# Attention ahead of two expert layers on one Trainium2 core: the first batch entry's values and the written order of its attention

## The chip, the cores and the metric

One core of one Trainium2 chip. The metric is the device time of one execution in microseconds (us). The kernel's engines: TensorE multiplies matrices (PE in the profile; its weight loads are PEld), VectorE (DVE) and ScalarE (ACT) work on tiles in SBUF and PSUM, GpSimd (POOL) on SBUF alone, and SyncE (SP) issues all the loads and stores of this kernel, in one queue.

## The reference

Three parts follow one another; the change touches the first alone.

```python
B, H, S, D = 2, 8, 576, 64            # q, k, v: (B, H, S, D); factor 4, Sd = 144
q_d, k_d, v_d = means over groups of 4 positions
out_d = softmax(scale * q_d @ k_d.T) @ v_d          # coarse, repeated 4 times
mask = abs(i - j) < 4                               # a band of 7
out_local = softmax(where(mask, scale * q @ k.T, -1e9)) @ v
x = out_up + out_local                              # as (1152, 512)
# then: 8 experts, relu(x @ w1[e]) @ w2[e], weighted by a gate that is normalised
# 8 times by rows and columns; then softplus(h @ w_in) @ w_out, h the experts' sum
```

## The kernel before

**Attention.** A `Unit` is two heads of one batch entry; there are eight, four for each entry (b = 0, then b = 1). Each has four blocks: "c", the coarse attention, and 0, 1, 2, the local attention of three tiles of 64 queries each, every tile against its window of 72 keys. `units` lists them, and the loop over n at line 746 runs through the 32 blocks. For block n it emits the scores of block n, the transposes of the weights of block n - 2 (`turn`), and the products with the values of block n - 3 (`values`). The next unit's `setup` stands in the third and fourth block of a unit, the `load` of the unit after it in the fourth.

`load` (line 291) issues on SyncE the queries and keys of two heads (`qk`, one place, four loads), the local values by windows (`vw`, two places, four loads) and the values for the coarse part (`vd`, one place, two loads). `setup(g)` transposes three tiles on TensorE into a PSUM bank, sums groups of four on VectorE (line 327), and copies queries and keys to `flat`, `kT` and `fine`. For g = 0 GpSimd also adds the values of each group of four (lines 345 and 346) into `vs`. `scores` runs the matmuls, then VectorE takes the row maximum (374) and scales it (375), ScalarE takes three exponentials with their sums (379), and VectorE adds, inverts and multiplies (384 to 388). `values` runs the matmuls with `vs` (419) or `vw` (429), and VectorE adds both parts (444). When a unit of the first entry has its last block, `operands` makes from `xf` the seven operands for a dense product, each split in two parts of lower precision (240 to 242).

**Dense work.** `fetch_first` and `fetch_second` load a piece of w1 or w2 into `raw` (two places), and ScalarE, VectorE and GpSimd split it in two parts, with sums for a scheme of seven products in place of eight (111, 132 to 139, 153, 154). `first` is that product (line 606), `second` the second layer's (665). `beside` is the dense work of the first four steps on the first entry's rows; it is emitted among the second entry's blocks, from n = 19 on, 3600 columns a block. `hh` and `hl` hold the hidden layer and are first used there, two places each. After the attention comes the rest of the dense work, in which TensorE's order is written out by hand.

**Order.** Outside blocks marked `tc.manual_schedule(engines=...)` a planner chooses each engine's order from costs of its own; each engine then works through its list in that order. Inside, the engines named keep the order in which the program emits their instructions. The three stretches in the loop that belong to the first entry's attention are all the planner's: SyncE's loads, TensorE's matmuls, and the other engines' work.

Of the kernel before, what the change touches and what calls it, by code (L numbers as in the profile page):

```python
# [9 lines left out]
F32 = mybir.dt.float32  # L10
# [3 lines left out]
AF = mybir.ActivationFunctionType  # L14
# [6 lines left out]
def attention_moe_mlp(ctx: ExitStack, tc: tile.TileContext, q, k, v, w_gate, w1, w2, w_in, w_out, out):  # L21
    nc = tc.nc
# [13 lines left out]
    KD = DM // P  # L36
    SCALE = 1.0 / float(D) ** 0.5
    EPS = 1e-9
    NEG = -1e9 / SCALE

# [235 lines left out]
    class Unit:  # L278
# [2 lines left out]
        pairs = {}  # L281

        def __init__(self, n, b, u):
            self.b, self.u = b, u
            self.flat = flat[n % 2]
            self.state = {}

# [3 lines left out]
        def load(self, first=False):  # L291
            b, h0 = self.b, 2 * self.u
            self.qk = qk = ap.tile([P, NQ, 2, D], F32, tag="qk", bufs=1, name="qk")
            cuts = [slice(NB * g, NB * g + NB) for g in range(NB)] if first else [slice(0, NQ)]
            for cut in cuts:
                for w, src in enumerate((q, k)):
                    for hh in range(2):
                        nc.sync.dma_start(
                            qk[w * QT : (w + 1) * QT, cut, hh],
                            src[b, h0 + hh].rearrange("(t p) d -> p t d", p=QT)[:, cut],  # L300
                        )
            self.vw = vw = ap.tile([KW, NQ, 2, D], F32, tag="vw", name="vw")
            for t, w0 in ((0, 0), (NQ - 1, S - KW)):
                nc.sync.dma_start(vw[:, t], v[b, h0 : h0 + 2, w0 : w0 + KW, :].rearrange("h p d -> p h d"))
            for hh in range(2):
                src = v[b, h0 + hh, QT - R :, :]
                windows = bass.AP(tensor=src.tensor, offset=src.offset, ap=[[D, KW], [QT * D, NQ - 2], [1, D]])
                nc.sync.dma_start(vw[:, 1 : NQ - 1, hh], windows)
            self.vd = vd = ap.tile([HC, 2, 2, R, D], F32, tag="vd", bufs=1, name="vd")
            for hh in range(2):  # L310
                nc.sync.dma_start(vd[:, :, hh], v[b, h0 + hh].rearrange("(c p r) d -> p c r d", c=2, r=R))

        def setup(self, g):

            if g == 0:
                self.kT = ap.tile([P, NQ, QT], F32, tag="kT", name="kT")
                self.qkd = ap.tile([P, NQ, 2, QT // R], F32, tag="qkd", name="qkd")
            qkd = self.qkd
            tb = self.bank("tb", 1)
            tiles = slice(NB * g, NB * g + NB)  # L320
            for j in range(NB):
                nc.tensor.transpose(
                    tb[:, j * P : (j + 1) * P], self.qk[:, NB * g + j].rearrange("p h d -> p (h d)"), ident
                )
            tb = tb[:, : NB * P]
            tbv = tb.rearrange("x (t w p) -> x t w p", t=NB, w=2)
            nc.vector.tensor_reduce(  # L327
                qkd[:, tiles].rearrange("x t w g -> x (t w) g"),
                tb.rearrange("x (t g r) -> x t g r", g=QT // R, r=R), axis=AX.X, op=ALU.add,
            )  # L330
            for hh in range(2):
                half = slice(hh * D, (hh + 1) * D)
                nc.vector.tensor_copy(
                    self.flat[half, g, hh].rearrange("x (j g) -> x j g", j=NB), qkd[half, tiles, 0]
                )
            nc.scalar.copy(self.kT[:, tiles], tbv[:, :, 1])
            nc.vector.tensor_copy(fine[g][:D, :, 0], tbv[:D, :, 0])
            nc.scalar.copy(fine[g][D:, :, 1], tbv[D:, :, 0])
            if g:
                return  # L340
            vd = self.vd

            self.vs = vs = ap.tile([HC, 2, 2, D], F32, tag="vs", name="vs")
            for c in range(2):
                nc.gpsimd.tensor_tensor(vd[:, c, :, 0:2, :], vd[:, c, :, 0:2, :], vd[:, c, :, 2:4, :], op=ALU.add)
                nc.gpsimd.tensor_tensor(vs[:, c], vd[:, c, :, 0, :], vd[:, c, :, 1, :], op=ALU.add)

        def scores(self, blk):

            sc = self.bank("sc", 0)  # L350
            if blk == "c":
                rows, w, scale = 2 * CT, SD, SCALE / (R * R)
                for i in range(NB):
                    nc.tensor.matmul(
                        sc[:rows, i * w : (i + 1) * w], self.flat[:, i].rearrange("x h q -> x (h q)"),
                        self.qkd[:, :, 1], start=True, stop=True,
                    )
            else:
                rows, w, scale = P, KW, SCALE
                tiles = range(NB * blk, NB * blk + NB)  # L360
                nc.tensor.matmul(
                    sc[:, : NB * w], identb, mask[:, blk : blk + NB].rearrange("p t w -> p (t w)"),
                    start=True, stop=False,
                )
                for i, t in enumerate(tiles):
                    w0 = min(max(t * QT - R, 0), S - KW)
                    nc.tensor.matmul(
                        sc[:, i * w : (i + 1) * w], fine[blk][:, i].rearrange("x h q -> x (h q)"),
                        self.kT.rearrange("x t q -> x (t q)")[:, w0 : w0 + KW], start=False, stop=(i == NB - 1),
                    )  # L370
            scv = sc[:rows, : NB * w].rearrange("p (i s) -> p i s", i=NB)
            small = ap.tile([P, 3, NB, 1], F32, tag="small", bufs=4, name="small")
            mx, off, rs = [small[:rows, i] for i in range(3)]
            nc.vector.tensor_reduce(mx, scv, axis=AX.X, op=ALU.max)
            nc.vector.tensor_scalar(off, mx, -scale, None, op0=ALU.mult)
            ex = ap.tile([P, NB * SD], F32, tag="ex", bufs=3, name="ex")[:rows, : NB * w]
            ex = ex.rearrange("p (i s) -> p i s", i=NB)
            for i in range(NB):
                nc.scalar.activation(
                    ex[:, i], scv[:, i], AF.Exp, scale=scale, bias=off[:, i], accum_out=rs[:, i]  # L380
                )
            if blk == "c":

                nc.vector.tensor_scalar(rs, rs, EPS, float(R), op0=ALU.add, op1=ALU.mult)
            else:
                nc.vector.tensor_scalar(rs, rs, EPS, None, op0=ALU.add)
            nc.vector.reciprocal(rs, rs)
            nc.vector.tensor_tensor(ex, ex, rs.to_broadcast([rows, NB, w]), op=ALU.mult)
            self.state[blk] = ex
# [22 lines left out]
        def values(self, blk):  # L412
# [2 lines left out]
            pv = self.bank("pv", 2)  # L415
            if blk == "c":
                for hh in range(2):
                    for c in range(2):
                        nc.tensor.matmul(
                            pv[hh * D : (hh + 1) * D, :SD], self.vs[:, c, hh],  # L420
                            et[:, c].rearrange("s (i h q) -> s i h q", i=NB, h=2)[:, :, hh],
                            start=(c == 0), stop=(c == 1),
                        )
                self.xc = ap.tile([P, SD], F32, tag="xc", name="xc")
                nc.scalar.copy(self.xc, pv[:, :SD])
                return
            for i in range(NB):
                for hh in range(2):
# [27 lines left out]

    units = [Unit(4 * b + i, b, u) for b in range(B) for i, u in enumerate((0, 2, 1, 3))]
    units[0].load(first=False)

    wg = const.tile([P, 3, 2, E], F32, name="wg")  # L460
    nc.sync.dma_start(
# [277 lines left out]
    for g in range(NB):  # L739
        units[0].setup(g)  # L740
    units[1].load()
    LAG = 2
    DENSE = 3600
    side, columns = beside(), 0
    begin = len(stream) // 2 + LAG
    for n in range(len(stream) + LAG + 1):
        if n < len(stream):
            x, blk = stream[n]
            i, j = divmod(n, len(blocks))
            x.scores(blk)  # L750
            if j == 1 and 1 <= i <= 6:
                (fetch_first if i % 2 else fetch_second)((i - 1) // 2, (i - 1) // 2)
            if j >= 2 and i + 1 < len(units):
                for g in ((0, 1), (2,))[j - 2]:
                    units[i + 1].setup(g)
                if j == 3 and i + 2 < len(units):
                    units[i + 2].load()
        for lag, what in ((LAG, "turn"), (LAG + 1, "values")):
            if 0 <= n - lag < len(stream):
                x, blk = stream[n - lag]  # L760
                getattr(x, what)(blk)
        while columns < (n - begin) * DENSE:
            columns += next(side, 1 << 30)
    for _ in side:
# [99 lines left out]
```

## Time and profile before

| | us |
|---|---|
| median of 3 runs | 1100.37 (1095.17 to 1103.46) |
| the profiled execution's own time | 1101.04 |
| its span, first to last instruction | 1099.3 |
| TensorE busy | 1059.5 |
| VectorE busy | 731.5 |
| ScalarE busy | 555.6 |
| GpSimd busy | 540.4 |

Busy time is summed from the records of instructions. Those of TensorE overlap, so two records of 0.28 us can start 0.12 us apart; start to start tells what one costs. The clock column (PEclk) is the clock granted to TensorE in parts of 2.4 GHz: 1.00, or 0.50 for 1.2 GHz, or a mean of both.

### The profile page before, as it was taken

Reading aid. Unit: us, or ns where it says so; the run is one execution under the profiler, and the core shown is the slowest. Engines: PE = TensorE matmul, PEld = TensorE weight load, DVE = VectorE, ACT = ScalarE, POOL = GpSimd, SP = SyncE. Lnnn points to the kernel's source line nnn. Section 1 sums busy time; section 2 is a strip of 40 time slices with the busy share of each in tenths; the row PEclk is TensorE's granted clock in tenths of the full one; section 3 lists DMA queues with packets and bytes.
Section 4 is the critical chain, followed back from the end, with each engine's and each line's share of the span. In section 5 each row is a group of like instructions: output and inputs, shape, how many; then the busy total and the mean of one; then the engine's idle time right before and its main releaser. Section 6 shows DMA issues by size and latency. Waiting matters only on the chain.

```text
span 1099.3 us, 17902 instructions
## 1 busy us (share of the span) xinstructions
PE 1059.5 (96%) x6385; PEld 936.9 (85%) x6385; DVE 731.5 (67%) x1564; ACT 555.6 (51%) x1443; POOL 540.4 (49%) x569
## 2 busy tenths in 40 slices
PE   6699999999999999999999999999999998999998
PEld 5588878898987889888888988888898897889987
DVE  6999666565666676667667565766663578766765
ACT  4677644443444344434444443444443567676763
POOL 6745244565467576757765455354664212322321
PEclk9779989999999999999999999999999999999999
DMA  7545111211234335333443333223333273244112
GB/s 174 119 110 119 38 32 39 77 58 40 65 118 142 113 101 154 116 120 115 122 133 105 117 113 98 97 96 108 103 116 115 106 278 140 110 173 182 68 39 86
DMA packets 133497, 119.70 MB, mean 109 GB/s; under 512 B 35744, under 2 KB 111776, under 8 KB 133408
## 3 DMA queue, kind: packets, MB, share of 16 engines
q1 hardware_dynamic: 133408, 118.56, 35.0%
q8 instruction: 50, 0.82, 0.3%
q14 instruction: 39, 0.32, 0.1%
HBM read 93.11 MB, written 25.43 MB: 108 GB/s over the span
## 4 chain that ended last, share of the span: by engine, by line
PE 39%; POOL 5%; DMA 5%; DVE 4%; issue 3%; ACT 2%; SPq 0%; POOLq 0%; DVEq 0%; ACTq 0%
PE yps L665 20%; PE m L606 18%; DMA raw<-in_moe_w_out 2%; POOL sums L111 2%; POOL w2l L154 1%; POOL cva L188 1%; DMA raw<-in_moe_w 1%; POOL cva L197 1%; DMA raw<-in_moe_w_in 1%; DVE cva L178 1%; POOL w1l L139 1%; DVE cva L189 0%; DVE cva L179 0%; DVE cva L182 0%; ACT raw L196 0%
## 5 line engine op out<-in xcount | busy, mean ns | idle before, releaser
L606 PE MATMUL m<-xh,w1h 128*128 128x320 f32 (+1 forms) x1120 | 336.7, 301 | 13.2 <-ACT t L615 7.3
L606 PE MATMUL m<-xl,w1h 128*128 128x320 f32 (+1 forms) x1120 | 332.6, 297 | 0.0
L606 PE MATMUL m<-xh,w1l 128*128 128x320 f32 (+1 forms) x1120 | 332.2, 297 | 0.0
L606 PEld LDWEIGHTS m<-xh,w1h 128*128 128x128 f32 x1120 | 212.1, 189 | 38.8 <-ACT t L615 11.6
L606 PEld LDWEIGHTS m<-xl,w1h 128*128 128x128 f32 x1120 | 212.3, 190 | 12.0 <-DVE qkd L327 0.2
L606 PEld LDWEIGHTS m<-xh,w1l 128*128 128x128 f32 x1120 | 212.2, 189 | 0.3 <-issue 0.2
L665 PE MATMUL yps<-w2h,hh 128*128 128x512 f32 x502 | 198.6, 396 | 1.2 <-ACT hh L563 1.2
L665 PE MATMUL yps<-w2l,hh 128*128 128x512 f32 x502 | 198.2, 395 | 0.0
L665 PE MATMUL yps<-w2h,hl 128*128 128x512 f32 x502 | 196.4, 391 | 0.0
L665 PE MATMUL yps<-w2h,h 128*128 128x512 f32 x436 | 152.8, 392 | 0.0
L620 DVE TENSOR_TENSOR c<-m,t 128x256 f32<-128x256 f32 (+1 forms) x160 | 72.2, 452 | 98.1 <-PE m L606 96.7
L139 POOL TENSOR_TENSOR w1l<-sums,w1h 128x512 fp32r<-128x512 f32 x72 | 95.5, 1340 | 78.6 <-ACT w1h L138 57.7
L154 POOL TENSOR_TENSOR w2l<-raw,w2h 128x512 fp32r<-128x512 f32 x72 | 95.5, 1348 | 74.8 <-ACT w2h L153 74.8
L576 POOL TENSOR_TENSOR ab<-ab,up 128x320 f32<-128x320 f32 (+1 forms) x64 | 53.9, 843 | 157.9 <-ACT ln L572 114.5
L563 ACT ACTIVATE hh<-c 128x256 fp32r<-128x256 f32 (+1 forms) x138 | 60.1, 443 | 126.1 <-DVE c L620 123.4
L564 DVE SCALAR_TENSOR_TENSOR hl<-c,hh 128x256 fp32r<-128x256 f32 (+1 forms) x138 | 91.8, 671 | 35.3 <-ACT hh L563 33.3
L665 PEld LDWEIGHTS yps<-w2h,hl 128*128 128x128 f32 x502 | 94.5, 188 | 22.0 <-DVE hl L564 0.4
L665 PEld LDWEIGHTS yps<-w2h,hh 128*128 128x128 f32 x502 | 94.9, 189 | 13.7 <-ACT hh L563 1.5
L682 DVE SCALAR_TENSOR_TENSOR acc<-yps,pr,acc 128x512 f32<-128x512 f32 x117 | 86.9, 743 | 29.3 <-PE yps L665 29.2
L665 PEld LDWEIGHTS yps<-w2l,hh 128*128 128x128 f32 x502 | 94.9, 189 | 10.7
L665 PEld LDWEIGHTS yps<-w2h,h 128*128 128x128 f32 x436 | 82.2, 189 | 14.7
L188 POOL TENSOR_TENSOR cva<-cva,raw 128x512 uint32<-128x512 uint32 x32 | 42.8, 1338 | 95.1 <-DVE raw L185 76.6
(136 smaller groups left out, 1708.6 us busy)
## 6 DMA issues: line engine op xcount, KB each, us to landing
raw<-in_moe_w SPq DMA_DIRECT2D x72, 256.0 KB
raw<-in_moe_w SPq DMA_DIRECT2D x36, 512.0 KB
w1h<-s_in SPq DMA_DIRECT2D x10, 896.0 KB
w1l<-s_in SPq DMA_DIRECT2D x10, 896.0 KB
raw<-in_moe_w_in SPq DMA_DIRECT2D x32, 256.0 KB
raw<-in_moe_w_out SPq DMA_DIRECT2D x16, 512.0 KB
w2l<-s_out SPq DMA_DIRECT2D x10, 512.0 KB
w2h<-s_out SPq DMA_DIRECT2D x10, 512.0 KB
```

The source lines that it names most:

```text
L111: nc.gpsimd.tensor_tensor(sums[i], a, b, op=op)
L139: nc.gpsimd.tensor_tensor(lo[:, part], sums, hi[:, part].bitcast(F32), op=ALU.subtract)
L154: nc.gpsimd.tensor_tensor(lo[:, i], raw[:, i], hi[:, i].bitcast(F32), op=ALU.subtract)
L178: nc.vector.tensor_scalar(a, high, 0x07FFFFFF, 3, op0=ALU.bitwise_and, op1=ALU.logical_shift_left)
L188: nc.gpsimd.tensor_tensor(a, a, low, op=ALU.add)
L563: nc.scalar.activation(hh, c, AF.Relu)
L564: nc.vector.scalar_tensor_tensor(out=hl, in0=c, scalar=0.0, in1=hh.bitcast(F32), op0=ALU.max, op1=ALU.subtract)
L576: nc.gpsimd.tensor_tensor(ab, ab, up, op=ALU.subtract)
L606: nc.tensor.matmul(b[:, :h], x[:, i, kk, :], y[s][:, i, kk, :], start=(not more and n == 0), stop=(n == 5), skip_group_check=more,)
L620: nc.vector.tensor_tensor(c, b[:, :h], t, op=ALU.add)
L665: nc.tensor.matmul(y, a[:, f, tok], b[:, f, :], start=(start and m == 0), stop=(stop and m == 5))
L682: nc.vector.scalar_tensor_tensor(out=acc[t], in0=y, scalar=pr[:, t, e : e + 1], in1=acc[t], op0=ALU.mult, op1=ALU.add,)
```

## The change

The diff, cut to what changes the work:

```diff
-    NEG = -1e9 / SCALE
+    NEG = -1e9
 ...
 class Unit: load()
+            if b:
+                self.vd = vd = ap.tile([HC, 2, 2, R, D], F32, tag="vd", bufs=1, name="vd")
+            else:
+                vd = hp.tile([P, 4 * HALF[1]], F32, tag=("hh", "hl")[self.n % 2], name="vd0")
+                self.vd = vd = vd[:HC, : 4 * R * D].rearrange("p (c h r d) -> p c h r d", c=2, h=2, r=R)
+            for hh in range(2):
+                nc.sync.dma_start(vd[:, :, hh], v[b, h0 + hh].rearrange("(c p r) d -> p c r d", c=2, r=R))
+
+        def load_windows(self):
+            b, h0 = self.b, 2 * self.u
             self.vw = vw = ap.tile([KW, NQ, 2, D], F32, tag="vw", name="vw")
 ...
-            self.vd = vd = ap.tile([HC, 2, 2, R, D], F32, tag="vd", bufs=1, name="vd")
-            for hh in range(2):
-                nc.sync.dma_start(vd[:, :, hh], v[b, h0 + hh].rearrange("(c p r) d -> p c r d", c=2, r=R))
 setup()
-                nc.vector.tensor_copy(
-                    self.flat[half, g, hh].rearrange("x (j g) -> x j g", j=NB), qkd[half, tiles, 0]
+                nc.vector.tensor_scalar(
+                    self.flat[half, g, hh].rearrange("x (j g) -> x j g", j=NB), qkd[half, tiles, 0],
+                    SCALE / (R * R), None, op0=ALU.mult,
                 )
-            nc.scalar.copy(self.kT[:, tiles], tbv[:, :, 1])
+            nc.scalar.mul(self.kT[:, tiles], tbv[:, :, 1], SCALE)
 ...
-            if g:
+            if g or not self.b:
                 return
 scores()
-            nc.vector.tensor_reduce(mx, scv, axis=AX.X, op=ALU.max)
-            nc.vector.tensor_scalar(off, mx, -scale, None, op0=ALU.mult)
+            nc.vector.tensor_reduce(off, scv, axis=AX.X, op=ALU.max, negate=True)
 ...
-                nc.scalar.activation(
-                    ex[:, i], scv[:, i], AF.Exp, scale=scale, bias=off[:, i], accum_out=rs[:, i]
-                )
-            if blk == "c":
-                nc.vector.tensor_scalar(rs, rs, EPS, float(R), op0=ALU.add, op1=ALU.mult)
-            else:
-                nc.vector.tensor_scalar(rs, rs, EPS, None, op0=ALU.add)
+                nc.scalar.activation(ex[:, i], scv[:, i], AF.Exp, bias=off[:, i], accum_out=rs[:, i])
+            nc.vector.tensor_scalar(rs, rs, EPS, None, op0=ALU.add)
 values(), coarse
-                    for c in range(2):
+                    terms = [
+                        (c, x) for c in range(2)
+                        for x in ([self.vs[:, c, hh]] if self.b else [self.vd[:, c, hh, r] for r in range(R)])
+                    ]
+                    for m, (c, x) in enumerate(terms):
 ...
-                nc.scalar.copy(self.xc, pv[:, :SD])
+                nc.scalar.mul(self.xc, pv[:, :SD], 1.0 / R)
 the loop
-    for n in range(len(stream) + LAG + 1):
+    def block(n):
+        i, j = divmod(n, len(blocks))
 ...
-            if j == 1 and 1 <= i <= 6:
-                (fetch_first if i % 2 else fetch_second)((i - 1) // 2, (i - 1) // 2)
+            for f, fetch in {
+                1: [(0, fetch_first)], 3: [(0, fetch_second)], 6: [(1, fetch_first)],
+                9: [(1, fetch_second)], 14: [(2, fetch_first)], 18: [(2, fetch_second)],
+            }.get(n, []):
+                fetch(f, f)
 ...
+        if j == 2 and 1 <= i < len(units) - 1:
+            units[i + 1].load_windows()
+
+    with tc.manual_schedule(engines={mybir.EngineType.PE, mybir.EngineType.SP}):
+        for n in range(begin):
+            block(n)
+    for n in range(begin, len(stream) + LAG + 1):
+        block(n)
         while columns < (n - begin) * DENSE:
```

For the first entry the values of the coarse part go to the places of `hh` and `hl`, one of four for each unit, and stay as loaded; the sum over a group of four happens in the PSUM accumulation, with four matmuls for each one of before, and the factor 1/4 in the copy behind. The second entry keeps one place and GpSimd's sums. The factor of the scores goes into the copies of the transposed queries' means and keys, and the maximum's sign into its reduction. Loads of windows are apart from `load` and stand in the third block of the unit before. The pieces of weights are fetched at blocks 1, 3, 6, 9, 14 and 18 instead of 5, 9, 13, 17, 21 and 25. TensorE and SyncE follow the written order in the first 18 blocks.

## Rows read from the trace of the kernel before

**Rows 1.** The page, part 1: busy time (share of the span) xinstructions.

```profile
PE 1059.5 (96%) x6385; PEld 936.9 (85%) x6385; DVE 731.5 (67%) x1564; ACT 555.6 (51%) x1443; POOL 540.4 (49%) x569
```

**Rows 2.** Windows of 20 us: length, each engine's busy time, granted clock, DMA.

```profile
0.00:20.00 20.00, 11.80 (x53) 10.38 (x54) 10.72 (x35) 8.55 (x32) 10.71 (x32) 1.00 0.81 175
20.00:40.00 20.00, 14.89 (x104) 11.97 (x104) 18.63 (x49) 14.66 (x55) 16.30 (x19) 0.88 0.55 136
40.00:60.00 20.00, 14.07 (x96) 11.71 (x95) 18.72 (x46) 10.44 (x42) 14.31 (x16) 0.59 0.57 109
60.00:80.00 20.00, 19.91 (x172) 17.07 (x171) 17.77 (x64) 14.48 (x63) 6.54 (x9) 0.77 0.61 133
80.00:100.00 20.00, 18.49 (x179) 16.17 (x178) 19.72 (x68) 16.58 (x65) 8.94 (x11) 1.00 0.40 89
...
140.00:160.00 20.00, 18.44 (x118) 13.47 (x117) 14.52 (x26) 9.51 (x30) 8.87 (x10) 0.83 0.04 13
```

**Rows 3.** Windows cut by unit (columns: PE, PEld, DVE, ACT, POOL, clock).

```profile
11.36:27.14 15.78, 13.42 (x61) 11.09 (x62) 13.82 (x36) 10.44 (x42) 9.78 (x13) 1.00 0.90 200
27.14:42.10 14.96, 11.51 (x92) 9.32 (x93) 13.59 (x41) 10.52 (x42) 11.47 (x13) 0.77 0.57 128
42.10:62.26 20.16, 14.23 (x98) 11.71 (x97) 18.92 (x43) 11.64 (x46) 14.52 (x18) 0.58 0.54 113
62.26:74.16 11.90, 11.81 (x96) 10.19 (x94) 10.99 (x42) 7.66 (x36) 3.65 (x6) 0.70 0.52 111
74.16:85.86 11.70, 10.78 (x116) 9.34 (x115) 10.32 (x41) 9.73 (x39) 2.63 (x5) 1.00 0.55 124
```

**Rows 4.** VectorE's groups by shape, 0 to 70.3 us.

```profile
L386 DVE TENSOR_SCALAR small<-small 128x3 f32<-128x3 f32 x9 | 6.5, 719 | 0.1
...
L375 DVE TENSOR_SCALAR small<-small 128x3 f32<-128x3 f32 x11 | 4.2, 390 | 0.0
...
L375 DVE TENSOR_SCALAR small<-small 96x3 f32<-96x3 f32 x4 | 3.8, 942 | 0.0
```

**Rows 5.** Lines 375 and 333, whole span: duration ns min/median/max.

```profile
L375 DVE TENSOR_SCALAR small<-small x32: 149/169/2455, 13.9 to 140.7; 128x3 f32<-128x3 f32 x24, 96x3 f32<-96x3 f32 x8
...
L333 DVE COPY flat<-qkd x48: 181/198/202, 8.3 to 122.9; 64x48 f32<-64x48 f32 x48
```

**Rows 6.** Timelines of DVE, POOL and PE, 47 to 52 us: start, length.

```profile
47.74 2.52 DVE L375 TENSOR_SCALAR small<-small 96x3 f32<-96x3 f32 x2
...
48.09 1.40 POOL L111 TENSOR_TENSOR sums<-raw 128x256 f32<-128x256 f32 x2
...
51.55 0.34 PE L361 MATMUL sc<-mask,identb 128*128 128x216 bf16 x1 [4.46 <-ACT ex L379]
```

**Rows 7.** GpSimd's groups by shape, 0 to 70.3 us: the value sums.

```profile
L345 POOL TENSOR_TENSOR vd<-vd 72x256 f32<-72x256 f32 x12 | 8.5, 726 | 12.7 <-DMA vd<-in_v 12.7
...
L346 POOL TENSOR_TENSOR vs<-vd 72x128 f32<-72x128 f32 x10 | 4.8, 488 | 0.2 <-PE pv L419 0.2
```

**Rows 8.** TensorE's timeline, 58 to 62 and 84 to 88.2 us.

```profile
60.26 1.24 PE L419 MATMUL pv<-etc,vs 72*64 72x144 f32 x8
61.43 0.86 PE L408 MATMUL tp<-ident,ex 128*72 128x128 f32 x3
...
84.86 0.72 PE L419 MATMUL pv<-etc,vs 72*64 72x144 f32 x8 [0.43 <-ACT fine L338]
85.51 0.39 PE L606 MATMUL m<-xl,w1h 128*128 128x256 f32 x1
```

**Rows 9.** Window of the first unit, line 419 alone: PE, PEld, clock, DMA.

```profile
11.36:27.14 15.78, 1.97 (x8) 1.05 (x8) 1.00 0.90 200
```

**Rows 10.** Waits in the first 150 us, GpSimd's and the SP queue's.

```profile
POOL vd L345 <- DMA vd<-in_v: 23.0, 7, 5.5
...
SPq L304 <- PE pv L429: 41.3, 6, 12.3
```

**Rows 11.** Window of line 606 alone: PE, PEld, clock, DMA.

```profile
70.30:82.00 11.70, 4.60 (x22) 3.15 (x22) 1.00 0.46 106
```

More of the change, by code (lines that the diff above doesn't have):

```diff
@@ L283, in __init__ @@
         def __init__(self, n, b, u):
-            self.b, self.u = b, u
+            self.n, self.b, self.u = n, b, u
             self.flat = flat[n % 2]
@@ L351, in scores @@
             if blk == "c":
-                rows, w, scale = 2 * CT, SD, SCALE / (R * R)
+                rows, w = 2 * CT, SD
                 for i in range(NB):
@@ L358, in scores @@
             else:
-                rows, w, scale = P, KW, SCALE
+                rows, w = P, KW
                 tiles = range(NB * blk, NB * blk + NB)
@@ L371, in scores @@
             scv = sc[:rows, : NB * w].rearrange("p (i s) -> p i s", i=NB)
-            small = ap.tile([P, 3, NB, 1], F32, tag="small", bufs=4, name="small")
-            mx, off, rs = [small[:rows, i] for i in range(3)]
-            nc.vector.tensor_reduce(mx, scv, axis=AX.X, op=ALU.max)
-            nc.vector.tensor_scalar(off, mx, -scale, None, op0=ALU.mult)
+            small = ap.tile([P, 2, NB, 1], F32, tag="small", bufs=4, name="small")
+            off, rs = [small[:rows, i] for i in range(2)]
+            nc.vector.tensor_reduce(off, scv, axis=AX.X, op=ALU.max, negate=True)
             ex = ap.tile([P, NB * SD], F32, tag="ex", bufs=3, name="ex")[:rows, : NB * w]
@@ L417, in values @@
                 for hh in range(2):
-                    for c in range(2):
+                    terms = [
[3 more added lines that the diff above has]
+                    for m, (c, x) in enumerate(terms):
                         nc.tensor.matmul(
-                            pv[hh * D : (hh + 1) * D, :SD], self.vs[:, c, hh],
+                            pv[hh * D : (hh + 1) * D, :SD], x,
                             et[:, c].rearrange("s (i h q) -> s i h q", i=NB, h=2)[:, :, hh],
-                            start=(c == 0), stop=(c == 1),
+                            start=(m == 0), stop=(m == len(terms) - 1),
                         )
                 self.xc = ap.tile([P, SD], F32, tag="xc", name="xc")
-                nc.scalar.copy(self.xc, pv[:, :SD])
+                nc.scalar.mul(self.xc, pv[:, :SD], 1.0 / R)
                 return
@@ L458, in attention_moe_mlp @@
     units[0].load(first=False)
+    units[0].load_windows()
     wg = const.tile([P, 3, 2, E], F32, name="wg")
@@ L741, in attention_moe_mlp @@
     units[1].load()
+    units[1].load_windows()
     LAG = 2
@@ L745, in attention_moe_mlp @@
     begin = len(stream) // 2 + LAG
-    for n in range(len(stream) + LAG + 1):
+    def block(n):
+        i, j = divmod(n, len(blocks))
         if n < len(stream):
             x, blk = stream[n]
-            i, j = divmod(n, len(blocks))
             x.scores(blk)
-            if j == 1 and 1 <= i <= 6:
-                (fetch_first if i % 2 else fetch_second)((i - 1) // 2, (i - 1) // 2)
+            for f, fetch in {
[3 more added lines that the diff above has]
+                fetch(f, f)
             if j >= 2 and i + 1 < len(units):
```

## The prediction

> **What bounds the kernel now.** I began with the busy shares. TensorE is busy 1059.5 of 1099.3 us [rows 1], so a change pays only where TensorE idles or runs at its lower clock. The table by 20 us says where: the idle time of the first five slices is 8.20, 5.11, 5.93, 0.09 and 1.51 us, 20.8 in all [rows 2], against 40 in the whole span. Apart from the wait for the first loads this is the first entry's attention, which the change rewrites.
>
> Then the same table cut by head pairs. I cut where the coarse scores (line 354) of each unit begin, so a row is the pace of one unit [rows 3]: 15.78, 14.96, 20.16 and 11.90 us for the first entry's four (62.8 in all), 11.70 for the next. In the first three VectorE is busy 13.82 of 15.78, 13.59 of 14.96 and 18.92 of 20.16 us: it sets the pace. GpSimd's busy time moves with the pace: 9.78, 11.47 and 14.52 us in the slow units, 3.65 and 2.63 in the two fast ones.
>
> Why GpSimd matters is seen in VectorE's groups by shape. The two tiny scalings of line 375 and the addition of line 386 write 3 columns and take 390, 942 and 719 ns on average [rows 4], while the median of line 375 is 169 ns and its longest 2455 [rows 5]. One of these waits can be read off: at 47.74 two of them take 2.52 us together, GpSimd runs sums from 48.09 to 49.49 with more behind, and TensorE sits idle for 4.46 us until the exponentials that want line 375's result are done [rows 6]. So a tiny VectorE instruction waits behind GpSimd, and TensorE behind it.
>
> The Trainium skill (SBUF — State Buffer, Who interferes with whom) names this: copies and tensor-scalar instructions that use two ports wait for GpSimd's whole instruction. The trace agrees (2455 ns against 169).
>
> **The change, part by part.** *Line 375 goes*, since the reduction of line 374 negates its maximum. In the first 70.3 us 15 of them take 4.2 + 3.8 = 8.0 us [rows 4]. Own cost is 15 x 0.169 = 2.5 us; 5.5 us is waiting. Part of the waiting will be met by the next instruction that GpSimd can block (lines 386, 388); I take half, 2.7 us, as met again. Gain on VectorE 8.0 - 2.7 = 5.3 us, bounds 2.5 and 8.0, over some 3.75 units: 1.4 us a unit.
>
> *GpSimd's value sums go* for four units: two of line 345 at 726 ns and two of line 346 at 488 [rows 7] are 2.4 us a unit, 9.7 in all (the other 4 and 2 in those rows are the second entry's, and stay). GpSimd's busy time in the four units is 39.4 us [rows 3]; 29.7 stay, weight splits above all, 7.4 us a unit. Pace against GpSimd's time: the mean of the fast two is 11.8 us at 3.1, of the slow three 17.0 at 11.9, a slope of 0.59 us per us. At 7.4 it gives 11.8 + 0.59 x 4.3 = 14.3 us. This slope holds part of the waiting that I counted with line 375, so I take 1.0 of the 1.4 us there: 13.3 us a unit, bounds 11.8 (the quiet units) and 15.0 (the fastest slow one).
>
> *TensorE takes the sums*: 16 matmuls for 4, so 24 records more a unit. Eight take 1.17 us from start to start at 60.26, at 1.2 GHz, and 0.65 at 84.86, at 2.4 [rows 8]: 0.146 or 0.081 each, 3.5 or 1.95 us a unit. While VectorE sets the pace this costs nothing; TensorE's idle time in the first 60 us covers it. Without cover it costs 7.8 to 14 us in four units. In the first unit there is no cover. The clock column reads 1.00 there, but eight such records took 1.97 us [rows 9], even more than at 60.26, so I read that stretch as 1.2 GHz. TensorE is busy 13.42 us in it; with 3.5 more, 16.9 us.
>
> *Four places for the values* end waits on GpSimd (23.0 us in the first 150 [rows 10]), which only fed the sums: nothing on the path. *The windows' loads* come three blocks later, in a written order. Now their issue waits 41.3 us for TensorE on the SP queue [rows 10]; behind it stand the next head pair's query and key, and the weights. In the written order the wait for the values matmul stands right behind that matmul; what is queued behind it is the next unit's load. I cost this at 0; if a load came late, the transposes would wait, for as long as the worst stall that the rows show, 4.46 us [rows 6].
>
> *The weight fetches* move to blocks 1, 3, 6, 9, 14 and 18. Their conversions cost ScalarE, VectorE and GpSimd what they did: 0. *The scale* goes into copies that are there already. The copy of line 333 becomes a tensor-scalar, six a unit. Line 333 took 181 to 202 ns in all 48 [rows 5], so GpSimd never blocked it, and I take the new form at the same time; at worst each waits as line 386 does, 719 - 169 = 550 ns [rows 4, 5], 3.3 us a unit.
>
> *The written order of TensorE*: its waits stand now where a planner put them. A block later or earlier is worth some us either way; the rows have no price for it but the stalls that it may add or end (idle 5.11 and 5.93 us per slice [rows 2]). I take 0, with 5 us to each side.
>
> *What is given back.* Before, 22 records of the dense first product ran between 70.30 and 82.00 in gaps of the attention [rows 11]: they are busy 4.60 us there, but overlap; 256 columns at 2.4 GHz are 0.107 us, 22 of them 2.3 us. I expect the written order not to take them in; they come later, at full price.
>
> **The sum**: 16.9 + 3 x 13.3 = 56.8 us against 62.8, 6.0 less; 2.3 given back; 3.7 us gained, since all behind is bound by TensorE and only shifts. The profiled execution took 1101.04 us, 1.7 of it outside the span; 1097.3 follows. It lies 0.67 above the median of the runs, so on their scale 1096.7. No change and 1% (11 us) can hardly be told apart here.
>
> **Rivals.** *TensorE takes VectorE's place at the lower clock.* The granted clock fell (0.77, 0.58) in the two units where TensorE was busy 11.51 of 14.96 and 14.23 of 20.16 us, and was 1.00 in the one where it was busy 10.78 of 11.70 [rows 3]; a unit of 13.3 us leaves it gaps again. At 1.2 GHz a unit needs 14.23 + 3.5 = 17.7 us, above 13.3. If half of the last three units runs so, they take 15.5 each: 16.9 + 46.5 = 63.4, 0.6 more and 2.3 given back, 1103 on the runs' scale. If all of it does: 16.9 + 3 x 17.7 = 70.0, 7.2 more and 2.3 given back, 1110. This is the case on the other side; it decides if the clock stays low past the second unit. For it: 24 more records a unit on an engine that is slow there. Against it: a TensorE that never idles was given 1.00 in the end (60 to 80 us: busy 19.91 of 20, clock 0.77, then 1.00) [rows 2].
>
> *The clock rises early and stays.* If the denser stream gets 2.4 GHz in the second unit and the long stalls as at 47 us are gone, the units run at the pace of the quiet two: 16.9 + 3 x 11.8 = 52.3, 10.5 less; if the dense records still find gaps, nothing is given back, and the hole at 140 to 160 us (1.56 us idle, clock 0.83 [rows 2]) closes: 12.1 us less, 1088.3. The Trainium skill (TensorE: Matmul & The Clock Gate, Part 1) speaks for this: "the default state is throttled, and activity releases the throttle." The trace agrees in the slices from 60 us on.
>
> *The change doesn't do what it says*: line 333 in its new form is blocked like line 386, 3.3 us a unit on VectorE. 13.3 + 3.3 = 16.6, sum 66.7, 6.2 more with what is given back: 1106.6. The Trainium skill (VectorE: DVE Perf Modes, Mode 2×_2P) puts copy and tensor-scalar under one condition, on where the operands lie and how they are cut; by it, the new form does as the copy did, and nothing is added.
>
> **How the numbers follow.** Forecast 0.40 (1096.7; own range 1091.7 to 1101.7, the 5 us of the written order to each side); TensorE the bound half of the time 0.20 (1103); low clock throughout 0.13 (1110); early clock 0.21 (1088.3); blocked line 333 0.06 (1106.6). With the same 5 us about the two far cases, the range leaves out their outer parts: 1085 to 1110. Faster by over 1% (under 1089.4): most of the early clock and a little of the forecast, 0.22. Slower by over 1% (over 1111.4): the outer part of the low clock and late loads, 0.10. Within: 0.68.
>
> **What will show it.** The distances of the coarse scores' starts: 17, then about 13 us. VectorE without line 375; line 374 as long as before; line 333 at 0.2 us; line 386 still long where GpSimd splits weights. GpSimd's busy time near 7.4 us a unit. The coarse values' matmuls at 32 records a unit, 2.6 us at 2.4 GHz or 4.7 at 1.2. The first dense records, now scattered from 70.30 on, begin near there again, in a closed stream. I am wrong if a unit takes over 15 us, if TensorE waits for a load, or if the stretch after 100 us changes by more than what I shift.

## The result, and the profile after

The changed kernel takes 1108.78 us (median of 20 runs, 1099.26 to 1116.04) against 1100.80 us for the kernel before on the same chip (20 runs, 1095.17 to 1104.64): a ratio of 1.0059, 95% interval 1.0041 to 1.0077. It is slower, by 8.0 us between the medians; I had predicted 4 us less. Ten of its runs lie between 1099 and 1107 us and ten between 1111 and 1116. The profiled execution is one of the lower ten: 1102.99 us, with a span of 1101.2 against 1099.3.

The page, parts 1 and 3, shows more on TensorE and less on the two engines that were relieved [rows 1]: 96 records of matmuls (two for each of 48) and 96 of weight loads more, VectorE 10 us and GpSimd 13 us less. The queue marked q8 instruction has 51 packets in place of 50; it matters below.

```profile
PE 1064.5 (97%) x6481; PEld 944.2 (86%) x6481; DVE 721.5 (66%) x1532; ACT 555.1 (50%) x1443; POOL 527.3 (48%) x553
...
q8 instruction: 51, 0.84, 0.3%
```

Windows by unit, cut at the starts of the coarse scores (now line 363), answer to [rows 3]:

```profile
10.49:27.58 17.09, 16.93 (x78) 15.16 (x78) 10.62 (x37) 11.05 (x42) 8.35 (x8) 1.00 0.93 193
27.58:44.52 16.94, 16.14 (x121) 14.01 (x120) 11.95 (x37) 10.65 (x42) 5.91 (x7) 1.00 0.29 61
44.52:56.86 12.34, 11.38 (x120) 9.91 (x119) 10.75 (x38) 10.21 (x43) 2.64 (x2) 1.00 0.61 140
56.86:70.21 13.35, 12.97 (x132) 11.48 (x132) 12.70 (x40) 11.60 (x46) 8.94 (x11) 1.00 0.79 177
70.21:83.41 13.20, 11.20 (x113) 9.23 (x111) 12.56 (x36) 8.95 (x39) 7.72 (x10) 0.98 0.65 153
```

The first four units take 59.7 us in place of 62.8. In the first two VectorE is busy 10.62 and 11.95 us and TensorE 16.93 of 17.09 and 16.14 of 16.94: TensorE is the bound now. Where that time goes is one row a unit in TensorE's timeline (start, length, with the row that follows):

```profile
20.60 7.04 PE L426 MATMUL pv<-etc,vd 72*64 72x144 f32 x32
27.58 0.80 PE L363 MATMUL sc<-qkd,flat 128*96 128x144 f32 x2
...
40.88 3.70 PE L426 MATMUL pv<-etc,vd 72*64 72x144 f32 x32
44.52 0.98 PE L363 MATMUL sc<-qkd,flat 128*96 128x144 f32 x6
```

The 32 records of the coarse values take 6.98 us from their start to the next row's in the first unit, and 3.64 us in the second: 0.218 and 0.114 us a record, where I had taken 0.146 and 0.081 from eight of them [rows 8].

A landmark splits the rest. The first matmul of the gates (tile lt), which weight the experts, stands where the attention is over. Tile lt, before (line 480) and after (line 489), with the third execution of the changed kernel, e6, below them in a fence of its own (duration ns, first and last start):

```profile
L480 PE MATMUL lt<-xh,wgs x16: 308/354/415, 147.4 to 157.7; 128*16 128x256 f32 x8, 128*16 128x320 f32 x8
```

```profile
L489 PE MATMUL lt<-xh,wgs x16: 276/300/313, 144.5 to 154.4; 128*16 128x256 f32 x8, 128*16 128x320 f32 x8
```

```profile
L489 PE MATMUL lt<-xh,wgs x16: 276/300/313, 155.9 to 165.7; 128*16 128x256 f32 x8, 128*16 128x320 f32 x8
```

The profiled execution reaches the gates 2.9 us ahead of the kernel before, close to the 3.7 us of the forecast. From there to the end of the span it needs 1101.2 - 144.5 = 956.7 us, and the kernel before 951.9. So two things have to be explained: why other executions reach the gates late, and why all three profiled ones lose some 5 us behind the gates, where the program has hardly changed.

### The profile page after: what moved, and what is told of

The parts are those of the page before. It is cut to its first block, busy times and chain, and to the rows that moved or that the text cites. A ratio compares the mean times of both kernels' runs of the same rounds, so it can differ in the third digit from the quotient of the medians.

```text
span 1101.2 us, 18049 instructions
## 1 busy us (share of the span) xinstructions
PE 1064.5 (97%) x6481; PEld 944.2 (86%) x6481; DVE 721.5 (66%) x1532; ACT 555.1 (50%) x1443; POOL 527.3 (48%) x553
## 4 chain that ended last, share of the span: by engine, by line
PE 38%; POOL 5%; DMA 5%; DVE 5%; issue 3%; ACT 2%; SPq 0%; POOLq 0%; ACTq 0%; DVEq 0%
PE yps L674 20%; PE m L615 18%; DMA raw<-in_moe_w_out 2%; POOL sums L111 1%; DMA raw<-in_moe_w 1%; POOL cva L188 1%; POOL w2l L154 1%; POOL cva L197 1%; DVE cva L178 1%; DVE cva L179 1%; POOL w1l L139 1%; DVE cva L189 0%; DMA s_out<-cva 0%; DVE cva L182 0%; DMA s_in<-cva 0%
```

## The experiments

Ratios are to the kernel before, run on the same chip. "Gates" is the first matmul of tile lt in the run's profile, "behind" the span less that.

### The order of the two heads, and the written order

**e1, the two heads in turn.** The change runs eight matmuls (sixteen records) for one head, then eight for the other; here they alternate. The sums are the same.

```diff
-                for hh in range(2):
-                    for m, (c, x) in enumerate(terms):
+                terms = [(c, r) for c in range(2) for r in range(1 if self.b else R)]
+                for m, (c, r) in enumerate(terms):
+                    for hh in range(2):
+                        x = self.vs[:, c, hh] if self.b else self.vd[:, c, hh, r]
```

> The changed kernel, with the coarse values' matmuls of the two heads in turn instead of one head's sixteen records after the other's. Theory A (the added matmuls cost more than priced, because one head's matmuls stand in a row and those of the other head, which write the other half of the output's partitions, can't run beside them): 32 records take about 2.0 us at 2.4 GHz and 3.9 at 1.2 instead of 3.7 and 7.0; the dense stream starts 6 to 9 us earlier than in the changed kernel; the median falls from 1108.8 to 1100 to 1103. Rival B (what is gained ahead of 160 us is lost again in the later stages, where the order of instructions is the same): the dense stream starts earlier, the median stays at 1106 to 1110.

Measured: 1098.11 us, ratio 0.9976 (0.9949 to 1.0002), some 9 us faster than the change by the ratios, and not to be told from the kernel before. TensorE's timeline of e1, the same 32 records at the lower clock and at the higher:

```profile
36.01 4.11 PE L423 MATMUL pv<-etc,vd 72*64 72x144 f32 x32
40.05 0.56 PE L363 MATMUL sc<-qkd,flat 128*96 128x144 f32 x1
...
49.57 2.18 PE L423 MATMUL pv<-etc,vd 72*64 72x144 f32 x32
51.68 0.36 PE L363 MATMUL sc<-qkd,flat 128*96 128x144 f32 x1
```

They take 4.04 and 2.11 us: 0.126 and 0.066 us a record, little over half of what they cost in a row. The heads write PSUM partitions 0 to 63 and 64 to 127; in turn, records of the two start in pairs (at 49.742 and 49.747, 49.864 and 49.870 in e1), while those of one head start one by one, 0.12 us apart (at 41.059, 41.181, 41.304 in the change; only where the two rows meet do they overlap, at 42.406 and 42.412). The Trainium skill (TensorE: Matmul & The Clock Gate, Why this matters for your kernels) says that small matmuls run concurrently when their outputs lie in distinct column groups (of 32 PSUM partitions there). The runs agree with halves of 64, and add that the order in the queue decides.

**e2, the planner's order in the changed kernel, and e8, the same with the heads in turn.** The written order is taken away; in e8 on top of e1's edit.

```diff
-    with tc.manual_schedule(engines={mybir.EngineType.PE, mybir.EngineType.SP}):
-        for n in range(begin):
-            block(n)
+    for n in range(begin):
+        block(n)
```

> The changed kernel without the written order of TensorE and SyncE in the first 18 blocks. If the written order costs the time: 1098 to 1102, units closer than 12 to 17 us. If it's the added matmuls (theory A): 1105 to 1112, the units no closer than in the changed kernel, since 32 records still take 3.7 us or more.

> The changed kernel with the two heads' matmuls in turn, and with TensorE's and SyncE's order left to the planner. Against the written order (1098.1 with the same matmuls): if the written order helps, 1100 to 1105; if it is neutral, 1097 to 1099; if it hurts, 1091 to 1095.

Measured: e2 1108.60 us, 1.0061 (1.0038 to 1.0084), as the change; e8 1106.24, 1.0037 (1.0024 to 1.0051). The written order is worth nothing with the heads in a row and some 7 us with the heads in turn (0.9976 against 1.0037; the two ran on different chips). The 5 us to either side that I allowed it did not hold for both.

### Parts alone

**e3, the small operations only**: the kernel before with the factor of the scores in the copies, the maximum negated in its reduction (line 375 gone) and the 1/4 in the copy behind. GpSimd sums the values and the planner orders.

```diff
-            nc.vector.tensor_reduce(mx, scv, axis=AX.X, op=ALU.max)
-            nc.vector.tensor_scalar(off, mx, -scale, None, op0=ALU.mult)
+            nc.vector.tensor_reduce(off, scv, axis=AX.X, op=ALU.max, negate=True)
```

> The kernel before, with only the scale and the negated maximum moved (line 375 goes, GpSimd's value sums, places, loads and order as before). If the waits of tiny VectorE instructions behind GpSimd set the pace of the first entry: units 1.0 to 1.4 us closer, the dense stream 3 to 5 us earlier, 1096 to 1098. If the gain is taken up later (rival B): dense stream earlier, time 1099 to 1102. If the waits only pass to the next instruction: no unit closer, 1100 to 1102.

**e4, TensorE's sums only**: the kernel before with the four places and the change's loop for the coarse values, heads in a row.

```diff
-            if g:
+            if g or not self.b:
                 return
...
+                    for m, (c, x) in enumerate(terms):
```

> The kernel before, with only the value sums of the first entry by TensorE and the four places for them. Theory A: GpSimd loses 2.4 us a unit, TensorE takes on 3.0 us a unit at 2.4 GHz and 5.8 at 1.2: 1104 to 1110. If GpSimd's relief outweighs it: 1094 to 1099.

**e7, all but TensorE's sums**: the changed kernel, with GpSimd adding the first entry's values again.

```diff
-            if g or not self.b:
+            if g:
                 return
...
-                        for x in ([self.vs[:, c, hh]] if self.b else [self.vd[:, c, hh, r] for r in range(R)])
+                        for x in [self.vs[:, c, hh]]
```

> The changed kernel, but the first entry's value sums are GpSimd's again (its four places, later windows, written order, moved scale stay). Theory A (TensorE's sums in a row are what costs): 1092 to 1097, as the small operations alone (1094.6) or better. If the written order or the later windows cost the time: 1099 to 1106.

Measured: e3 1094.63 us, 0.9953 (0.9930 to 0.9976), the fastest of all; e4 1109.89, 1.0085 (1.0055 to 1.0115); e7 1096.81, 0.9960 (0.9943 to 0.9976). So the small operations gain, more than any case that I had written down for them, and the sums on TensorE, heads in a row, cost more than that, as theory A says of e4 and e7. e4's windows by unit show TensorE as the bound of the first two:

```profile
11.35:28.43 17.08, 16.25 (x74) 13.88 (x73) 10.67 (x36) 9.84 (x41) 6.39 (x8) 1.00 1.07 205
28.43:45.05 16.62, 16.62 (x119) 14.55 (x119) 12.71 (x34) 11.02 (x42) 9.95 (x12) 1.00 0.52 101
```

In e3 the addition behind the exponentials, line 386 before [rows 4], takes 442 ns on average where it had 719, but the product behind it, line 388 before, takes 835 where it had 589. VectorE's groups by shape, 0 to 70 us, line 388 before and then e3:

```profile
L388 DVE TENSOR_TENSOR ex<-ex,small 128x216 f32<-128x216 f32 x9 | 5.3, 589 | 0.1
```

```profile
L382 DVE TENSOR_TENSOR ex<-ex,small 128x216 f32<-128x216 f32 x10 | 8.3, 835 | 0.1
...
L380 DVE TENSOR_SCALAR small<-small 128x3 f32<-128x3 f32 x11 | 4.9, 442 | 0.1
```

### The changed kernel's two levels

**e5 and e6, the changed kernel again**, one execution each.

> The changed kernel once more, for its profile: its executions fall into two groups, ten from 1099 to 1107 us and ten from 1111 to 1116. If this one is of the upper group: theory C (the lower clock lasts longer in the first entry's attention) has the gates' matmuls begin 8 to 11 us after the 144.5 us of the profile of the lower group, with more at 0.50 ahead of them; rival D (the later stages lose it) has them begin at 143 to 146 and the loss after 300 us.

> The same again, a third profile, to see an execution of either group: expectations as in the run before it.

Measured: 1107.56 us (e5) and 1114.74 us (e6). e5 lies between the two groups (gates at 147.3, 958.4 us behind). e6 is one of the upper ten's kind; its windows by unit:

```profile
10.12:23.82 13.70, 13.09 (x78) 11.97 (x78) 10.78 (x37) 10.34 (x41) 4.54 (x5) 1.00 0.98 186
23.82:42.29 18.47, 15.23 (x121) 12.93 (x120) 13.07 (x38) 11.00 (x44) 9.80 (x10) 0.76 0.65 147
42.29:62.81 20.52, 20.52 (x121) 17.94 (x120) 11.79 (x38) 10.59 (x42) 2.61 (x3) 0.50 0.40 79
62.81:80.55 17.74, 17.74 (x133) 15.84 (x133) 13.70 (x40) 12.63 (x48) 10.83 (x12) 0.68 0.37 89
```

Its units take 70.4 us. In the third TensorE is busy 20.52 of 20.52 us at a granted clock of 0.50, while VectorE needs 11.79. In the first profile that unit ran at 1.00 and took 12.34. The same program thus reaches the gates at 144.5 or at 155.9, and what differs is in which units TensorE's clock is up, much as theory C has it; why it differs from one execution to the next stays open. In the kernel before VectorE hid the lower clock in three units of four [rows 3]; its 20 runs lie within 10 us, the change's within 17.

### The loss behind the gates

The seven profiles so far with TensorE's sums need 955.5 to 958.4 us behind the gates; the kernel before needs 951.9, e3 950.2 and e7 954.4. In the changed kernel the loss is idle time of TensorE. Windows from the gates to the end, the kernel before and then the changed one, have it busy equally long (934.48 and 934.28 us):

```profile
147.40:1099.30 951.90, 934.48 (x5399) 831.46 (x5397) 611.24 (x1209) 461.83 (x1079) 464.26 (x466) 1.00 0.33 109
```

```profile
144.50:1101.20 956.70, 934.28 (x5404) 830.99 (x5400) 614.07 (x1211) 461.31 (x1080) 463.09 (x466) 1.00 0.33 108
```

It idles 17.4 and 22.4 us. Part of it can be read at 296 us. SyncE's queue (start, length of each issue), the kernel before and then the changed one:

```profile
299.70 0.34 SPq L216 DMA_DIRECT2D s_in<-cva  x1
300.09 0.45 SPq L217 DMA_DIRECT2D s_in<-cva  x1
301.20 0.36 SPq L215 DMA_DIRECT2D s_in<-sums  x1
```

```profile
296.29 0.34 SPq L216 DMA_DIRECT2D s_in<-cva  x1
296.68 1.70 SPq L217 DMA_DIRECT2D s_in<-cva  x1
298.43 0.46 SPq L215 DMA_DIRECT2D s_in<-sums  x1
...
q8 instruction: 1, 0.02, 3.6%
```

One issue takes 1.70 us in place of 0.45. The last line is from the table of DMA queues between 296.2 and 298.4 us: a packet of the queue marked instruction, 16 KB, which started at 296.71. In the kernel before that packet came at 295.64, ahead of the issues. What the late transfer holds up, in the changed kernel's timelines of GpSimd and of TensorE:

```profile
300.23 0.74 POOL L111 TENSOR_TENSOR sums<-raw 128x256 f32<-128x256 f32 x1 [2.47 <-DMA s_in<-cva]
...
306.89 0.39 PE L674 MATMUL yps<-w2h,hl 128*128 128x512 f32 x1
308.35 0.39 PE L615 MATMUL m<-xh,w1h 128*128 128x256 f32 x1 [1.07 <-DVE c L629]
```

GpSimd waits 2.47 us for the transfer, the weights' conversion is late, VectorE with it, and TensorE stands 1.07 us. The packets go with TensorE's records: 50 for 12770 before, one for each 255, so I take them for its program. The Trainium skill (Runtime: NRT & Kernel Launch, Instruction fetch mechanics) says that engines stream their instructions in blocks of 256, each crossing "mostly hidden". Here TensorE shows no idle time over 0.3 us in the 1 us behind any packet past the gates, but the transfer that starts with one is late. Behind the gates all six issues of the changed kernel that took over 0.3 us more than their kind (6.0 us in all), and both of the kernel before (1.6 us), have such a packet within 2 us; the packets come some 22 us apart.

The change adds 192 records ahead of all this, so all later packets fall elsewhere. e9 to e15 move them with matmuls that nobody reads.

**e9 to e11: padding in the first entry's units**, 8 a unit in e1's kernel (e9) and in the changed one (e11), 24 in e3's (e10).

```diff
+                if not self.b:
+                    for k in range(8):
+                        nc.tensor.matmul(pv[:D, SD : SD + 1], self.vd[:, 0, 0, 0], et[:, 0, :1], start=True, stop=True)
```

> The kernel of e1_halves_in_turn, with eight more matmuls of one column in front of the coarse values of each of the first entry's four units (32 in all, 64 records with their weight loads; nobody reads their column). Theory D (fetches of TensorE's program): the trace shows one packet of 16 KB on a queue marked instruction about every 256 records of TensorE, and behind the gates each issue on SyncE's queue that took over 0.3 us longer than its kind stands within 2 us of such a packet (two in the kernel before, six after, with 1.6 and 6.0 us of excess). The change's 192 records more shift all later packets by three quarters of a distance; 64 more complete the distance, so that behind the gates the packets stand where they stood in the kernel before. D expects 951 to 953 us from the first matmul of the gates to the end of the span (957.0 in e1, 951.9 before), and 1093 to 1095 us in all (1098.1 in e1). Rival P (the four places of the values, or the later stages' own phase against the weights, cost the 5 us): 956 to 958 us from the gates on, and 1098 to 1100 in all.

> The kernel of e3_small_ops_only (GpSimd's sums, planner's order, nothing of the places or of TensorE's sums), with 24 more matmuls of one column in front of the coarse values of each of the first entry's four units (96 in all, 192 records as in the change; nobody reads their column). Theory D: the later packets of TensorE's program shift as after the change, and from the first matmul of the gates to the end of the span it takes 955 to 958 us (950.2 in e3); in all 1099 to 1102 us (1094.6 in e3). Rival P: 950 to 952 us from the gates on, and 1094 to 1097 in all, the difference being what the 96 tiny matmuls cost in the first 75 us.

> The changed kernel as it stands, with the same eight matmuls of one column a unit as e9 (64 records more, so 256 more than the kernel before). Theory D: 951 to 953 us from the gates on (956.7, 958.4 and 957.2 in the three profiles of the changed kernel), and 4 to 5 us less in all: its runs then lie at 1095 to 1103 and 1106 to 1112 in place of 1099 to 1107 and 1111 to 1116. Rival P: 956 to 958 us from the gates on, and no difference in all but some 1 us more for the tiny matmuls.

Measured: e9 1106.12 us, 1.0061 (1.0040 to 1.0083); e10 1117.58, 1.0156 (1.0127 to 1.0185); e11 1116.79, 1.0146 (1.0115 to 1.0177). Every total is far above what either theory said (theory D: fetches of TensorE's program; rival P: the places of the values or the stages' own phase). The padding left four records a matmul, not two, and the first entry's units suffered: gates at 149.4 in e9 against 138.8 in e1, 154.7 in e10 against 142.5 in e3. Behind the gates the times moved as theory D says, 950.0, 957.5 and 951.9 us, but with 320, 384 and 320 records more in place of 256, 192 and 256, so this is no test of D.

**e12 to e15: padding in the second entry's units**, two records a matmul: 8 a unit in e1's kernel (e12) and the changed one (e14), 16 in e1's (e15), 24 in e3's (e13).

```diff
+                if self.b:
+                    for k in range(8):
+                        nc.tensor.matmul(pv[:D, SD : SD + 2], identb[:, :D], identb[:, :2], start=True, stop=True)
```

> The kernel of e1_halves_in_turn with 64 records more on TensorE, as e9 was meant, but in the second entry's units, where the clock is high: eight bf16 matmuls of two columns ahead of each unit's coarse values, two records each, nobody reads their columns. (In e9 to e11 each tiny float32 matmul left four records in place of two, and the first entry's units lost 10 us and more ahead of the gates, so the padding itself spoiled their totals.) Theory D (where the fetches of TensorE's program fall among the weights' transfers sets what is lost behind the gates): 256 records more than the kernel before, so the fetches fall as there; 950 to 954 us from the gates to the end (957.0 in e1), gates at 139 to 141, in all 1092 to 1096. Rival P: 956 to 958 us from the gates on, 1098 to 1101 in all.

> The kernel of e3_small_ops_only with 192 records more, as many as the change adds: 24 bf16 matmuls of two columns ahead of each coarse product of the second entry, nobody reads their columns. Theory D: fetches fall as after the change; 955 to 958 us from the gates on (950.2 in e3), in all 1099 to 1103 (1094.6 in e3). Rival P: 950 to 952 us from the gates on, in all 1095 to 1098, the difference being the 96 matmuls themselves.

> The changed kernel with the same 64 records more in the second entry's units as e12. Theory D: 950 to 954 us from the gates on (956.7, 958.4 and 957.2 in the changed kernel's three profiles), and 3 to 6 us less in all, its median near 1104. Rival P: 956 to 958 us from the gates on, its median at 1108 to 1110.

> The kernel of e1_halves_in_turn with 128 records more in the second entry's units (16 bf16 matmuls of two columns ahead of each coarse product), so that the fetches fall as in e9 and e11, which took 950.0 and 951.9 us from the gates on. Theory D: 949 to 953 us from the gates on, gates at 140 to 142, in all 1092 to 1096. Rival P: 956 to 958 us from the gates on, 1099 to 1102 in all.

Measured: e12 1097.77 us, 0.9965 (0.9944 to 0.9987); e13 1107.72, 1.0055 (1.0039 to 1.0070); e14 1104.63, 1.0026 (1.0005 to 1.0047); e15 1100.36, 0.9979 (0.9952 to 1.0007). Only two totals lie where a theory had them, each against its own time behind the gates: e14's total is D's and its time behind is P's, with e15 it is the other way round. The gates come at 148.1 in e12 (whose profile is the slowest of its twelve runs) and at 150.0 in e15, where I had 139 to 142. Ordered by the records that TensorE has beyond the kernel before (matmuls and loads, from the pages):

| records more | us behind the gates |
|---|---|
| 0 | before 951.9, e3 950.2, e7 954.4 |
| 192 | change 956.7, 958.4, 957.2; e1 957.0, e2 957.7, e4 956.6, e8 955.5, e13 958.2 |
| 256 | e12 956.5, e14 957.6 |
| 320 | e9 950.0, e11 951.9, e15 950.1 |
| 384 | e10 957.5 |

The clearest pair is e3 and e13. e13 is the fastest kernel with 96 idle matmuls; tile lt of each:

```profile
L474 PE MATMUL lt<-xh,wgs x16: 276/298/313, 142.5 to 151.5; 128*16 128x256 f32 x8, 128*16 128x320 f32 x8
```

```profile
L477 PE MATMUL lt<-xh,wgs x16: 276/299/312, 146.9 to 157.1; 128*16 128x256 f32 x8, 128*16 128x320 f32 x8
```

The spans are 1092.7 and 1105.1 us. Of the 12.4 us, 4.4 lie up to the gates (2.0 of them ahead of the first idle matmul, in units that are alike: the fifth starts at 71.58 and 73.53) and 8.0 behind, where nothing was added: 958.2 us, what the changed kernel takes. The four places of the values are not the cause, since e13 has none of them and loses, and e15 and e9 have them and don't.

Theory D fails too as I had put it. In e12 and e14, with 256 records more, each of the 42 packets behind the gates stands within 20 matmul records of one of the kernel before (half of them within 2), and they delay issues at the same places, within a line. One such pair, the kernel before and then e12:

```profile
387.58 1.36 SPq L216 DMA_DIRECT2D s_in<-cva  x1
```

```profile
389.46 1.78 SPq L217 DMA_DIRECT2D s_in<-cva  x1
```

They delay about as little: two issues in e12 and four in e14, 1.7 us in all in each, against two and 1.6. Yet both lost 5 us, in part in stalls of TensorE of 1.55 us at 627 and 1.35 at 622. And e15 has nine delayed issues (5.4 us in all), e11 eight (5.6) and e9 six (4.5), about what the changed kernel has, and they lost nothing. So the loss moves with the number of records ahead (192 against none or 320), and delayed issues explain single stalls, as the one at 308 us, but not the sum. Its cause stays open.

## Why the prediction was wrong

**The step that failed** is "TensorE takes the sums": 0.081 or 0.146 us a record, and "While VectorE sets the pace this costs nothing; TensorE's idle time in the first 60 us covers it." The price came from eight records that overlap [rows 8]: those at 84.86 start in pairs, at 84.865 and 84.878, 85.010 and 85.052, and so on. Sixteen of one head in a row don't: they took 0.114 and 0.218 us each, so a unit's 32 cost 3.64 or 6.98 us against the 2.6 or 4.7 that I named. And the cover was not there: with line 375 and GpSimd's sums gone VectorE needed 10.6 to 12.7 us a unit, and TensorE 16.9 and 20.5 in the two units that ran wholly at the lower clock (the first here, by the durations of its records, and the third of e6). That is the rival that I gave 0.20 and 0.13. Its far case, 70.0 us for four units, comes near e6's 70.4, in part by luck: the units are 13.7, 18.5, 20.5 and 17.7 us, not 16.9 and three times 17.7.

**VectorE** went as argued: busy 46.0 us in the four units in place of 57.3. With the small operations alone (e3) it is 53.7, 3.6 less, where I had 5.3 for line 375 with bounds of 2.5 and 8.0. Part of the waiting was met again, as I had said, at line 388 (835 ns, not 589). Units of 12.34 and 13.35 us at the higher clock answer to the 13.3 of the forecast, but TensorE is the busier engine in both (11.38 and 12.97 us, VectorE 10.75 and 12.70), so the number agrees and not the reason. GpSimd was busy 8.35, 5.91, 2.64 and 8.94 us in the units, 6.5 on average where I had 7.4.

**The first unit** took 17.09 us against 16.9, but by two errors that cancel: the coarse values were busy 7.04 us in place of 1.97 + 3.5, and the rest 16.93 - 7.04 = 9.89 us in place of 13.42 - 1.97 = 11.45. In e6, where the clock was up by 20 us and the 32 records took 3.70, it was 13.70 us.

**Line 333 in its new form** was never blocked; lines 333 before and 341 after have the same durations [rows 5]:

```profile
L341 DVE TENSOR_SCALAR flat<-qkd x48: 161/197/202, 8.6 to 121.8; 64x48 f32<-64x48 f32 x48
```

**The written order** I took as 0, 5 us to either side. Its worth depends on the order that is written: nothing as the change has it, some 7 us with the heads in turn.

**What is given back**, 2.3 us, did not come: 29 records of the dense product ran in the fourth and fifth units before (9 and 20 of line 606) and 29 after (12 and 17 of line 615).

**"All behind is bound by TensorE and only shifts"** is the second step that failed. In its place TensorE idled 5 us more behind the gates in the first profile, from a cause that stays open. The stretch cost 4.8 to 6.5 us in the three profiles, more than the 3.7 that I forecast as the gain. I had named it as a sign that I am wrong ("if the stretch after 100 us changes by more than what I shift"), with no chance beside it.

**The sum of the result**: in the first profile 2.9 us gained up to the gates and 4.8 lost behind, 1.9 on the span; in e6 8.5 us lost and 5.2 lost, 13.7 on the span. The twenty runs spread about these two, and their median, 8.0 us above that of the kernel before, falls between the two groups, where no run lies.

## What to carry to other kernels

Price an added matmul by records that stand in the order in which the new ones will stand: those of two column halves overlap in turn, those of one half don't. Before work is moved to an engine with idle time, ask who is the bound once the others are relieved, at the lowest clock that the profile shows for that engine. And when a stage in which nothing was changed moves by some us, pad the kernel with idle instructions before a story is made of it, and add up what the story explains: here the delayed transfers fitted the first profiles and not the padded ones.

## What the runs showed of the hardware

- Records of matmuls of 64 output partitions and 144 columns in distinct halves of PSUM's partitions, in turn: 0.066 us a record at 2.4 GHz and 0.126 at 1.2; in a row 0.114 and 0.218.
- A DMA issue on SyncE's queue took 1.70 us in place of 0.45 when a 16 KB packet of the queue marked instruction started with it.
- 96 idle matmuls made a kernel 1.0% slower (e3 to e13: 0.9953 to 1.0055); in the profiles 8.0 of 12.4 us lie in stages behind them. Why is open.
- A float32 matmul of one column left as many records as one of 144 (four, weight loads counted), and 32 of them among the first entry's matmuls went with a loss of 10.6 us up to the gates (e1 to e9, one profile each).
- The clock column reads 1.00 from the start to the first change on record, while the same matmuls have the durations of 1.2 GHz (6.98 us at 20.60, 3.64 at 40.88).
